# A queue of common PSUM banks, a fold cut in three, and a third bank for the last products

## The chip, the cores and the metric

The kernel runs on one core of one Trainium2 chip. The core has a matrix engine (PE, with a separate record PEld for its weight loads), a vector engine (DVE), a scalar engine (ACT), a general engine (POOL) and a queue engine (SP) that here issues nearly all transfers. PE writes its results into a memory of its own, PSUM, of which the kernel uses eight banks; DVE and ACT read them from there. The metric is the device time of one execution in microseconds.

## The reference, cut to what matters

The program computes a top-k attention and then a Fourier mixing block with a two-layer network. Everything is in 32-bit floats.

```python
scores = (1 / sqrt(64)) * q @ k^T                 # 8 batches, 8 heads, 576 x 576
kth = 32nd largest score of each row
attn = softmax(where(scores >= kth, scores, -1e9))
x = (attn @ v), heads side by side                # (8, 576, 512)

mixed = real(fft over 512 channels(fft over 576 tokens(x)))
u = x + mixed
un = (u - mean(u)) / sqrt(var(u) + 1e-6)
out = u + relu(un @ w_ch1) @ w_ch2                # 512 -> 2048 -> 512
```

## The kernel before, in words

**Steps and tiles.** The attention of the 32 pairs of heads is cut into 288 tiles, nine a pair and 36 a batch. The main loop at the end of the kernel takes one tile a step, in steps of about 6 us once it has settled. For tile i, DVE finds the 32 largest scores of each row with MAX8 and MATCH_REPLACE8 (`top_ops`, L384 and L386). POOL then forms two bounds from the first and last of them (`bounds`, L393, tile `nt`), ACT makes a mask (L400), POOL subtracts it from the scores (L401, tile `wk`), ACT takes the exponent (L407), PE transposes the result (L428, tile `tpP`), and matmuls with v follow (L465). These are spread over three consecutive steps: `bounds` of tile i in step i, mask and exponent in step i+1, transposes in step i+2.

**The second block rides along.** The Fourier mixing and the network of batch b are done while the attention of batch b+1 or b+2 runs. `at(step, where, fn)` books a piece of work for a place in a step. The list `queue` holds units of the network, and `some()` puts as many of them between the attention's matmuls as PE has room for by a cost in microseconds; only their order on PE is set by this, the semaphores do the rest. The units are, for each of two chunks of a batch (320 and 256 rows): 16 `hidden` units (L827, tile `hp`), then either plain products `back` (L854, tile `cp`; L893 for the 64 rows that are left over) or the seven products of a Strassen-Winograd scheme, `fast` (L1024, tiles `cv` and `cw`). Chunk 0 of batches 1 to 7 and chunk 1 of batch 7 are done by `fast`; batch 7 is the last.

**The common banks.** Three PSUM banks (pool `ps_m`) are shared by `hp`, `cp`, `cv`, `cw` and, in all but the last batch, by the transforms over tokens (`yp`, L629), over channels (`mp`, L677), the transposes before the network (`tpu`, L742) and some transposes of x (`tpx`, L505). The function `bank()` gives out the next one in turn, 0, 1, 2, 0, and so on. A tile that lives over many units is taken with `hold=True`; it is skipped in the turn until its `free` is called. A bank given out again while its former tile is still being read makes the new writer wait. In `back`, part 7 ends a `cp` tile: for row tile 2 ACT scales it into SBUF (L881), `free()` is called, and the next unit asks for the bank of row tile 3.

**The seven products.** In `fast`, two banks `v` and `w` are held. Each has a low and a high half of 256 columns. The products come as p2, p1, p5, p4, p6, p3, p7, each in two parts of four matmuls. p1, p6 and p7 add up in the low half of `w`; p4 is written into the high half of `w`. `to_x` adds a finished half to x: in the last batch directly from PSUM by DVE (L982), otherwise over ACT (L994) and POOL. `mix` (L969) makes sums of the hidden values on POOL, `bring` (L770) fetches parts of the second weight matrix over SP: p5 part n brings T2, which p6 part n uses.

**The fold.** Ahead of the transform over tokens, x is folded. `fold_tails(b, eng)` folds the 64 left-over rows of a batch: two adds of halves into `zt` (L566), then a memset, three copies and four adds into `ftail` (L550 to L562 and L575). For batches 1 to 6 it is booked as one call at place "pool0", which lies on POOL between the subtraction of tile i-1 (L401) and `bounds` of tile i (L393). `T0` is the step of the fold: the last step of the batch plus 3 for batch 1, plus 4 for batches 2 to 6. `fold_tails` stands at T0-1 for batch 1 and at T0 for batches 2 to 6; the large folds (`fold_ops`) follow from T0+1, and `yp` from T0+4 or T0+5.

Of the kernel before, what the change touches and what calls it, by code (L numbers as in the profile page):

```python
# [9 lines left out]
F32 = mybir.dt.float32  # L10
# [8 lines left out]
P = 128  # L19
# [45 lines left out]
def kernel(  # L65
# [9 lines left out]
    nc = tc.nc  # L75
    B, H, S, D = q.shape
    DM = H * D
# [5 lines left out]
    TAIL = 2 * TH  # L83
# [23 lines left out]
    batp = ctx.enter_context(tc.tile_pool(name="batp", bufs=1))  # L107
# [7 lines left out]
    ps_m = ctx.enter_context(tc.tile_pool(name="ps_m", bufs=3, space=bass.MemoryType.PSUM))  # L115


    held, turn = set(), [0]

    def bank(shape, name, hold=False):  # L120
        while turn[0] in held:
            turn[0] = (turn[0] + 1) % 3
        n = turn[0]
        turn[0] = (n + 1) % 3
        t = ps_m.tile(shape, F32, name=name, tag=f"m{n}", bufs=1)
        if not hold:
            return t
        held.add(n)
        return t, lambda: held.discard(n)

    ident = const.tile([P, P], F32, name="ident", tag="ident")
    fs = const.tile([P, 2, 2, 3, KQ], F32, name="fs", tag="fs")
# [11 lines left out]
    ftail = const.tile([P, DM + 1], F32, name="ftail", tag="ftail")  # L144
# [76 lines left out]
    x_of, o_of, xT_of, rd_of = ({} for _ in range(4))  # L221
# [322 lines left out]
    Q1, Q2, Q3 = DM // 4, DM // 2, 3 * DM // 4  # L544
    folded, y_of, yt_of, us_of, rs_of, unT_of = ({} for _ in range(6))

    def fold_channels(eng, z, f, n):

        def tt(out, up, down, op):
            eng.tensor_tensor(out=f[..., out], in0=z[..., up], in1=z[..., down], op=op)  # L550

        if n == 0:
            eng.memset(f[..., Q1:Q1 + 1], 0.0)
            eng.tensor_copy(out=f[..., 0:DM:Q2], in_=z[..., 0:DM:Q2])
            up, down = slice(1, Q1), slice(Q2 - 1, Q1, -1)
            tt(up, up, down, ALU.add)
            tt(slice(Q1 + 1, Q2), up, down, ALU.subtract)
        else:
            up, down = slice(Q2 + 1, Q3), slice(DM - 1, Q3, -1)
            tt(up, up, down, ALU.subtract)  # L560
            tt(slice(Q3, DM - 1), up, down, ALU.add)
            eng.tensor_copy(out=f[..., DM - 1:DM], in_=z[..., Q3:Q3 + 1])  # L562

    def fold_halves(eng, s_, z):
        for cols, op in ((slice(0, Q2), ALU.add), (slice(Q2, DM), ALU.subtract)):
            eng.tensor_tensor(out=z[..., cols], in0=s_[..., 0:Q2], in1=s_[..., Q2:DM], op=op)  # L566

    def fold_tails(b, eng):

        z = batp.tile([P, DM], F32, name=f"zt_{b}", tag="fold_s")[0:TAIL]  # L570
        f = ftail[0:TAIL]
        fold_halves(eng, x_of[b][0:TAIL, 4, :], z)
        for n in range(2):
            fold_channels(eng, z, f[:, 0:DM], n)
        eng.tensor_copy(out=f[:, DM:DM + 1], in_=z[:, Q1:Q1 + 1])  # L575

    def fold_ops(b, par, eng, space="own"):

# [234 lines left out]
    def mlp_units(b):  # L813
        x = x_of[b]
        last = b == B - 1
# [113 lines left out]
        def fast(ch):  # L929

            ta, tb = CHUNKS[ch][0], CHUNKS[ch][1]
# [12 lines left out]
            rs, banks = rs_of[b], {}  # L944
            lo, hi = slice(0, DH), slice(DH, DM)
# [8 lines left out]
            def room(n):  # L954
                return ct_tile().rearrange("p t c -> p (t c)")[:, DH * n:DH * (n + 1)]

            def later(key, us, fn, soon=False):

                n = sum(s[3] for s in sums) if soon else len(sums)
                sums.insert(n, ((b, ch, *key), us, fn, soon))  # L960
                if last:
                    need((b, ch, *key))
# [12 lines left out]
            def to_x(t, cols, src, n, then=lambda: None):  # L975


                xt = x[:, t, cols].rearrange("p (e c) -> p e c", c=DH)
                e = xt.shape[1]
                if n is None or last:  # L980
                    def add():
                        nc.vector.scalar_tensor_tensor(  # L982
                            out=xt,
                            in0=src.rearrange("p (e c) -> p e c", e=1).to_broadcast([P, e, DH]),
                            scalar=rs[:, t:t + 1], in1=xt, op0=ALU.mult, op1=ALU.add,
                        )
                        then()
                    if last:
                        add()
                    else:  # L990
                        late_next.append(add)
                    return
                r = room(n)
                nc.scalar.mul(out=r, in_=src, mul=rs[:, t:t + 1])  # L994
                xt = x[:, t, cols]
                later(("x", n), 0.75, lambda: nc.gpsimd.tensor_tensor(
                    out=xt, in0=xt, in1=r, op=ALU.add
                ))
# [20 lines left out]
            def product(name, cols, a, rhs_of, part, start):  # L1019


                dst = half_bank(name, cols)
                for kc in range(NK // 2 * part, NK // 2 * (part + 1)):
                    nc.tensor.matmul(  # L1024
                        dst, lhsT=h()[a][:, kc, :], rhs=rhs_of(kc), start=start and kc == 0,
                        stop=kc == NK - 1, skip_group_check=True,
                    )
                return dst
# [29 lines left out]
                    to_x(tb, hi, c, 2)  # L1058

            def p4(part):  # L1060
                c = product("w", hi, "22", in_second, part, False)
                bring(T3, second, part)
                if part:
                    to_x(tb, lo, c, 3)
                    mix("22", "22", "11")

            def p6(part):
# [92 lines left out]
    def at(step, where, fn, cost=0.0):  # L1160
        plan.setdefault((step, where), []).append(fn)
        costs[step] = costs.get(step, 0.0) + cost
# [68 lines left out]
    for o, place in ((B12, w2_12), (B21, w2_21)):  # L1231
        at(PER_BATCH + 14, "load2", lambda o=o, place=place: nc.sync.dma_start(
            out=scr[:, o], in_=place
# [3 lines left out]
    for b in range(B):  # L1237
        end = PER_BATCH * (b + 1) - 1
        last = b == B - 1
        first, soon = b == 0, b == 1  # L1240
        T0 = end + (2 if first else 3 if soon else 4)
        if first:

            at(T0 - 1, "pool", lambda b=b: fold_tails(b, nc.gpsimd))

            def folds(b=b):
                for par, space in ((0, "own"), (1, "hT")):
                    for op in fold_ops(b, par, nc.vector, space):
                        op()
            at(T0, "dve", folds)  # L1250
            ft, fc = (T0 + 1, T0 + 1), T0 + 1
        elif soon:

            at(T0 - 1, "pool0", lambda b=b: fold_tails(b, nc.gpsimd))
            for par in range(2):
                def folds(par=par, b=b, T0=T0):
                    for n, op in enumerate(fold_ops(b, par, nc.gpsimd)):
                        at(T0 + 1 + 3 * par + min(n, 2), "pool0", op)
                at(T0, "begin", folds)
            ft, fc = (T0 + 4, T0 + 7), T0 + 8  # L1260
        elif not last:
            at(T0, "pool0", lambda b=b: fold_tails(b, nc.gpsimd))
            for par in range(2):
                def folds(par=par, b=b, T0=T0):
                    for n, op in enumerate(fold_ops(b, par, nc.gpsimd)):
                        at(T0 + (6 if par else 1) + n, "pool0", op)
                at(T0, "begin", folds)
            ft, fc = (T0 + 5, T0 + 11), T0 + 12
        else:
            at(T0 - 1, "pool0", lambda b=b: fold_tails(b, nc.gpsimd))  # L1270

            def folds(b=b):
                for op in fold_ops(b, 0, nc.vector) + fold_ops(b, 1, nc.vector, "PT"):
                    op()
            at(T0, "dve", folds)

            at(T0 + 1, "pe1", lambda: one_unit() + one_unit() if len(queue) > 1 else 0.0)
            ft, fc = (T0 + 1, T0 + 3), T0 + 4
        for par in range(2):
            at(ft[par], "pe1", lambda b=b, par=par: dft_tokens(b, par), 4.3)  # L1280
        for n, t in enumerate((0, 1, 4, 2, 3)):
            quick = first or last
            s = fc + (0 if first else n // 3 if last else n // 2)
            at(s, "pe2", lambda b=b, t=t, q=quick: dft_channels(b, t, q), 1.75)
            if not quick:
                at(s, "pool2", lambda b=b, t=t: add_mixed(b, t))
                at(s + 1, "dve", lambda b=b, t=t: stats(b, t))
            at(s + (1 if quick else 2), "pe", lambda b=b, t=t: channels_first(b, t), 0.6)
            if first and t == 4:
                at(s + 1, "pe", lambda: (queue.extend(waiting), waiting.clear()) and 0.0)  # L1290
        at(s + 1, "begin" if quick else "dve", lambda b=b: rsqrt(b))
        arrivals.append(s + (1 if quick else 2))
        at(arrivals[-1], "units", lambda b=b: (queue if b else waiting).extend(mlp_units(b)))
# [43 lines left out]
    while i < N + 4 or plan or queue or sums:  # L1337
# [54 lines left out]
        cost, got = carry, 0.0  # L1392
# [38 lines left out]
        first, second = top_ops(i, (2, 3)), top_ops(i + 1, (0, 1))  # L1431
# [58 lines left out]
```

## Time and profile before

| what | value |
|---|---|
| median of 3 runs | 1923.65 us (1923.27 to 1925.76) |
| span of the profiled execution | 1923.6 us |
| PE busy | 1806.9 us, 94% of the span |
| DVE busy | 1585.2 us, 82% |
| ACT busy | 1210.0 us, 63% |
| POOL busy | 872.6 us, 45% |
| mean granted clock of PE | 0.973 |

All times within the run are microseconds from the start of the span. A line of the instruction listing gives the start, the time from the first to the last of a run of equal instructions, the engine, the line of the code, the operation, the tiles as out<-in with their shapes, and the number of instructions; in brackets stands the idle time of the engine before it and what ended it. A line of the list of waits gives who waited, for whom, the total, the number of times and the longest.

### The profile page before, as it was taken

How to read it: one execution, taken by the hardware profiler on the slowest of the kernel's cores; microseconds unless marked ns; L12 is line 12 of the kernel's file. 1: busy time of each engine (PE TensorE's matmuls, PEld its weight loads, DVE VectorE, ACT ScalarE, POOL GpSimd, SP SyncE). 2: the span in 40 equal slices, each digit the busy share in tenths (PEclk: the TensorE clock that was granted, in tenths of full speed). 3: DMA queues.
4: the chain of work that ended last, by engine and by line, in shares of the span. 5: the costliest groups of instructions: out<-in, count | busy, mean ns of one | idle time of the engine just before them, and what ended most of it. 6: DMA issues, size and time to landing. Idle time of an engine off the chain costs nothing.

```text
span 1923.6 us, 28279 instructions
## 1 busy us (share of the span) xinstructions
PE 1806.9 (94%) x9008; PEld 1195.3 (62%) x9008; DVE 1585.2 (82%) x3277; ACT 1210.0 (63%) x3078; POOL 872.6 (45%) x1158
## 2 busy tenths in 40 slices
PE   6567799999999999999999999999999999999999
PEld 3334465474666756667567656667567656767677
DVE  8999989999999998989899888888899988872110
ACT  6878657676766767656676667666676667652100
POOL 4768643545635364345535454345534454241012
PEclk8877899999999999999999999999999999999999
DMA  5333001220104111140013101140013102030132
GB/s 162 105 95 107 19 13 47 86 70 24 47 8 128 33 25 47 41 109 26 24 47 101 51 17 52 41 113 22 23 47 101 49 19 58 23 102 6 50 102 76
DMA packets 184339, 111.34 MB, mean 58 GB/s; under 512 B 125952, under 2 KB 174208, under 8 KB 184192
## 3 DMA queue, kind: packets, MB, share of 16 engines
q1 hardware_dynamic: 183408, 109.33, 20.0%
q8 instruction: 72, 1.18, 0.3%
q14 instruction: 75, 0.61, 0.1%
q10 hardware_dynamic: 784, 0.21, 0.0%
HBM read 93.76 MB, written 15.73 MB: 57 GB/s over the span
## 4 chain that ended last, share of the span: by engine, by line
PE 79%; POOL 6%; DVE 5%; ACT 4%; issue 3%; DMA 1%; SPq 0%; POOLq 0%; DVEq 0%; ACTq 0%
PE hp L827 25%; PE cp L854 11%; PE o L465 7%; PE sp L363 6%; PE tpP L428 5%; PE cw L1024 5%; PE cv L1024 4%; PE yp L629 3%; PE mp L677 3%; PE cp L893 3%; DVE m L384 3%; POOL wk L401 2%; DVE wk L386 2%; PE sp_t L333 2%; POOL w L215 1%
## 5 line engine op out<-in xcount | busy, mean ns | idle before, releaser
L401 POOL TENSOR_TENSOR wk<-S,wk 128x576 f32<-128x576 f32 x288 | 408.4, 1418 | 806.0 <-ACT wk L400 775.2
L384 DVE MAX8 m<-wk 128x8 f32<-128x576 f32 x864 | 623.3, 749 | 5.2
L827 PE MATMUL hp<-unT,w 128*128 128x256 f32 (+1 forms) x2048 | 538.3, 410 | 2.6 <-ACT unT L745 2.6
L827 PEld LDWEIGHTS hp<-unT,w 128*128 128x128 f32 x2048 | 373.6, 191 | 124.3 <-issue 24.2
L386 DVE MATCH_REPLACE8 wk<-m,wk 128x576 f32<-128x576 f32 x576 | 427.6, 742 | 0.0
L407 ACT ACTIVATE wk<-wk,nt 128x576 f32<-128x576 f32 x288 | 224.7, 780 | 66.4 <-POOL wk L401 65.5
L428 PE MATMUL tpP<-ident,wk 128*128 128x128 f32 x1152 | 184.6, 285 | 72.7 <-ACT wk L407 47.3
L854 PE MATMUL cp<-w,hT 128*128 128x512 f32 x512 | 242.6, 601 | 4.0 <-ACT hT L881 4.0
L431 ACT COPY PT<-tpP 128x512 f32<-128x512 f32 (+1 forms) x320 | 171.4, 546 | 118.8 <-PE tpP L428 116.4
L400 ACT ACTIVATE wk<-S,nt 128x576 f32<-128x576 f32 x288 | 226.9, 788 | 24.3 <-POOL nt L393 23.3
L428 PEld LDWEIGHTS tpP<-ident,wk 128*128 128x128 f32 x1152 | 141.6, 145 | 147.1 <-ACT wk L407 68.3
L831 ACT ACTIVATE hT<-hp 128x320 f32<-128x320 f32 (+1 forms) x256 | 104.9, 410 | 193.9 <-PE hp L827 191.8
L384 DVE MAX8 m<-S 128x8 f32<-128x576 f32 x288 | 214.0, 743 | 9.5 <-ACT S L337 9.4
L386 DVE MATCH_REPLACE8 wk<-m,S 128x576 f32<-128x576 f32 x288 | 213.7, 742 | 0.0
L465 PE MATMUL o<-PT,v 128*64 128x256 f32 (+3 forms) x1440 | 194.3, 412 | 1.5 <-ACT PT L431 1.4
L366 ACT COPY S<-sp 128x512 f32<-128x512 f32 (+1 forms) x264 | 141.9, 588 | 56.9 <-PE sp L363 56.5
L363 PE MATMUL sp<-kT,qT 64*128 64x512 f32 (+1 forms) x528 | 162.6, 675 | 4.3 <-ACT means L1210 3.3
L465 PEld LDWEIGHTS o<-PT,v 128*64 128x64 f32 x1440 | 111.1, 152 | 72.7 <-issue 15.8
L854 PEld LDWEIGHTS cp<-w,hT 128*128 128x128 f32 x512 | 89.0, 191 | 92.4 <-issue 85.7
L969 POOL TENSOR_TENSOR hT<-hT 128x512 f32<-128x512 f32 x64 | 81.5, 1276 | 101.1 <-ACT hT L831 89.4
L1024 PE MATMUL cw<-w,hT 128*128 128x256 f32 x448 | 106.5, 383 | 2.7 <-issue 1.4
L1024 PEld LDWEIGHTS cw<-w,hT 128*128 128x128 f32 x448 | 81.4, 190 | 20.3 <-issue 5.2
(140 smaller groups left out, 2150.2 us busy)
## 6 DMA issues: line engine op xcount, KB each, us to landing
w<-w_parts SPq DMA_DIRECT2D x82, 512.0 KB, 4.4
space<-in_moe_w_ch_dram SPq DMA_DIRECT2D x32, 512.0 KB, 3.5
nat<-in_q_dram SPq DMA_DIRECT2D x128, 64.0 KB, 2.2
v<-in_v_dram SPq DMA_DIRECT2D x128, 64.0 KB, 2.3
out_dram<-x SPq DMA_DIRECT2D x32, 256.0 KB, 2.1
nat<-in_k_dram SPq DMA_DIRECT2D x124, 64.0 KB, 2.2
w_parts<-w_t SPq DMA_DIRECT2D x8, 512.0 KB, 2.9
w_s<-w_parts SPq DMA_DIRECT2D x8, 512.0 KB, 4.9
```

Source lines behind the costliest of these rows:

```text
L363: nc.tensor.matmul(sp[r], lhsT=qT[hd, q_cols], rhs=kT[hd, :], start=True, stop=True)
L384: ops.append(lambda src=src, m8=m8: nc.vector.max(out=m8, in_=src))
L386: ops.append(lambda src=src, m8=m8: nc.vector.match_replace(w, m8, src, NEG))
L400: nc.scalar.activation(out=w, in_=Ssb[i], func=AF.Relu, scale=-FAR, bias=Nt[i][:, 1:2])
L401: nc.gpsimd.tensor_tensor(out=w, in0=Ssb.pop(i), in1=w, op=ALU.subtract)
L407: nc.scalar.activation(out=w, in_=w, func=AF.Exp, bias=Nt.pop(i)[:, 0:1], accum_out=den_t[pair % 3][:, c:c + 1],)
L428: nc.tensor.transpose(tp[:, c, :], p_sb[:, k0 + P * c:k0 + P * (c + 1)], ident)
L431: nc.scalar.copy(out=pt[:, NF * he:NF * (he + 1), col:col + w], in_=tp[:, :, o:o + w])
L465: nc.tensor.matmul(o[D * e:D * (e + 1), c0:c1], lhsT=vv[:, c, e, :], rhs=pt[:, 2 * NF if c == NF else NF * e + c, c0:c1], start=(c == 0), ...
L827: nc.tensor.matmul(hp[:, 0:w], lhsT=w1[:, dt, P * it:P * (it + 1)], rhs=unT[:, dt, 0:w], start=(dt == 0), stop=(dt == NDT - 1),)
L854: nc.tensor.matmul(cp, lhsT=hT[:, it, P * n:P * (n + 1)], rhs=w2[:, it, :], start=(it == 0), stop=(it == NIT - 1),)
L1024: nc.tensor.matmul(dst, lhsT=h()[a][:, kc, :], rhs=rhs_of(kc), start=start and kc == 0, stop=kc == NK - 1, skip_group_check=True,)
```

## The change

`bank()` keeps the free banks in a list: it takes the first, and a bank goes to the end of the list when it is given back, which for a tile taken without `hold` is at once. `fold_tails` returns three functions: the halves; the first half of the channels; the second half and the last copy. For batches 1 to 6 they are booked at T0-2, T0-1 and T0, one a step. For batches 0 and 7 all three stay in the step where the whole was. In the last batch p4 is written into a third held bank `z`, with the start flag on its first matmul, and `z` is given back when DVE has been told to add it to x.

Of the last two hunks of the diff the first is that of batch 1 and the second that of batches 2 to 6.

```diff
-    held, turn = set(), [0]
+    banks_free = [0, 1, 2]
     def bank(shape, name, hold=False):
-        while turn[0] in held:
-            turn[0] = (turn[0] + 1) % 3
-        n = turn[0]
-        turn[0] = (n + 1) % 3
+        n = banks_free.pop(0)
         t = ps_m.tile(shape, F32, name=name, tag=f"m{n}", bufs=1)
         if not hold:
+            banks_free.append(n)
             return t
-        held.add(n)
-        return t, lambda: held.discard(n)
+        return t, lambda: banks_free.append(n)
...
     def fold_tails(b, eng):
-        z = batp.tile([P, DM], F32, name=f"zt_{b}", tag="fold_s")[0:TAIL]
-        f = ftail[0:TAIL]
-        fold_halves(eng, x_of[b][0:TAIL, 4, :], z)
-        for n in range(2):
-            fold_channels(eng, z, f[:, 0:DM], n)
-        eng.tensor_copy(out=f[:, DM:DM + 1], in_=z[:, Q1:Q1 + 1])
+        f, got = ftail[0:TAIL], []
+        def first():
+            got.append(batp.tile([P, DM], F32, name=f"zt_{b}", tag="fold_s")[0:TAIL])
+            fold_halves(eng, x_of[b][0:TAIL, 4, :], got[0])
+        def third():
+            fold_channels(eng, got[0], f[:, 0:DM], 1)
+            eng.tensor_copy(out=f[:, DM:DM + 1], in_=got[0][:, Q1:Q1 + 1])
+        return [first, lambda: fold_channels(eng, got[0], f[:, 0:DM], 0), third]
...
             def p4(part):
-                c = product("w", hi, "22", in_second, part, False)
+                c = product("z" if last else "w", hi, "22", in_second, part, last)
                 bring(T3, second, part)
                 if part:
-                    to_x(tb, lo, c, 3)
+                    to_x(tb, lo, c, 3, lambda: banks["z"][1]())
...
-            at(T0 - 1, "pool0", lambda b=b: fold_tails(b, nc.gpsimd))
+            for n, op in enumerate(fold_tails(b, nc.gpsimd)):
+                at(T0 - 2 + n, "pool0", op)
...
-            at(T0, "pool0", lambda b=b: fold_tails(b, nc.gpsimd))
+            for n, op in enumerate(fold_tails(b, nc.gpsimd)):
+                at(T0 - 2 + n, "pool0", op)
```

More of the change, by code (lines that the diff above doesn't have):

```diff
@@ L1242 @@
         if first:
-            at(T0 - 1, "pool", lambda b=b: fold_tails(b, nc.gpsimd))
+            for op in fold_tails(b, nc.gpsimd):
+                at(T0 - 1, "pool", op)
             def folds(b=b):
@@ L1269 @@
         else:
-            at(T0 - 1, "pool0", lambda b=b: fold_tails(b, nc.gpsimd))
+            for op in fold_tails(b, nc.gpsimd):
+                at(T0 - 1, "pool0", op)
             def folds(b=b):
```

## The prediction

> **What bounds the kernel now.** I read four views in this order: the page (who is busy), the table by stage, the list of PE's waits, and the listing of instructions around each wait. The page and the table first:
>
> ```profile
> PE 1806.9 (94%) x9008; PEld 1195.3 (62%) x9008; DVE 1585.2 (82%) x3277; ACT 1210.0 (63%) x3078; POOL 872.6 (45%) x1158
> PE 79%; POOL 6%; DVE 5%; ACT 4%; issue 3%; DMA 1%; SPq 0%; POOLq 0%; DVEq 0%; ACTq 0%
> 0.00:250.00 250.00, 167.63 (x808) 103.34 (x809) 232.24 (x482) 187.31 (x441) 156.77 (x168) 0.81 0.31 94
> 250.00:800.00 550.00, 528.74 (x2661) 337.05 (x2660) 513.48 (x1058) 379.61 (x1000) 261.31 (x367) 0.99 0.17 47
> 800.00:1800.00 1000.00, 991.90 (x5030) 661.81 (x5029) 830.00 (x1722) 628.78 (x1603) 434.36 (x607) 1.00 0.19 53
> 1800.00:1924.00 124.00, 118.64 (x514) 93.09 (x512) 9.49 (x17) 14.30 (x34) 20.14 (x16) 1.00 0.22 71
> ```
>
> The first line is busy time by engine, the second the shares of the chain that ended last, the rest stages with PE, PEld, DVE, ACT and POOL. From 250 us on PE is the bound: 96% busy, then 99%, then 96%. Before 250 us DVE is (232 of 250), but nothing moves there: no bank is held before the first `back`, so both rules give 0, 1, 2, and batch 0 keeps its fold. A change that leaves PE's work alone can therefore win only PE's idle time after 250 us: 21.3 + 8.1 + 5.4 = 34.8 us. The order of PE's instructions is the same in both kernels except that p4 of the last batch goes to `cz`. So the question is which waits end.
>
> ```profile
> PE tpP L428 <- ACT wk L407: 10.8, 12, 3.7
> PE cp L854 <- ACT hT L881: 4.0, 4, 1.6
> PE tpu L742 <- ACT us L694: 1.5, 4, 0.4
> PE cw L1024 <- issue: 1.4, 3, 0.6
> ```
>
> These are PE's waits from 250 us to the end (total, times, longest). The second is a wait for a common bank, the first holds one wait of 3.7 us behind the fold, the last the two waits in the last batch. I take each to its place.
>
> [...] p6 (low half of `w`) starts at 1849.41, just after DVE's read of p4's high half (1848.83 + 0.48 = 1849.31). [...] matmuls that follow each other overlap by 0.16 us in the records (p4's start every 0.43, each 0.59 long), so a recorded gap costs 0.16 more than it shows; and `nt` stands behind a fold below. [...] the `cp` gap repeats once a batch.
>
> **Part 1, the queue of banks.** In batch 3:
>
> ```profile
> 1141.70 1.88 PE L854 MATMUL cp<-w,hT 128*128 128x512 f32 x4
> 1144.37 1.98 PE L854 MATMUL cp<-w,hT 128*128 128x512 f32 x4 [0.78 <-ACT hT L881]
> 1143.62 0.69 ACT L881 ACTIVATE hT<-cp,gi 128x512 f32<-128x512 f32 x1 [0.72 <-PE cp L854]
> ```
>
> Row tile 2 has just ended, ACT scales it out of its bank, and row tile 3 was given that very bank. Followed through the whole program, the two rules differ thus: `cp` of row tile 3 gets in batches 1 to 5 the bank of row tile 2 before, and after the change one whose last reader (L655, of `yp`) ended 10 to 21 us earlier. The four recorded gaps are 1.63 us (702.29, batch 1; ACT is late there, L881 runs 701.55 to 702.24) and 0.78 in batches 3, 4 and 5. In batch 2 row tile 3 starts at 927.11, after ACT was done, so nothing is won. With the overlap: 1.79 + 3 x 0.94 = **4.6 us**; the lower end is the gaps alone, 4.0. To see new waits I set, for every common bank after 250 us, the new predecessor's last read in this trace against the tile's first write. The four `tpu` waits stay (0.37 each, same predecessor `mp`); the closest new pair is `mp` of batch 1 at 498.38, 0.77 us after its new predecessor's last read. No wait is added.
>
> **Part 2, the fold in three.** Only batch 1 has a wait to win:
>
> ```profile
> 453.74 1.27 POOL L883 TENSOR_TENSOR x<-x,hT 128x512 f32<-128x512 f32 x1 [1.55 <-ACT hT L881]
> 454.97 1.41 POOL L566 TENSOR_TENSOR zt<-x 64x256 f32<-64x256 f32 x2
> 456.70 1.69 POOL L550 TENSOR_TENSOR ftail<-zt 64x127 f32<-64x127 f32 x4
> 458.59 0.18 POOL L393 TENSOR_TENSOR nt<-m,cc 128x2 f32<-128x2 f32 x1
> 458.81 0.78 ACT L400 ACTIVATE wk<-S,nt 128x576 f32<-128x576 f32 x1 [2.24 <-POOL nt L393]
> 462.02 0.66 PE L428 MATMUL tpP<-ident,wk 128*128 128x128 f32 x4 [3.68 <-ACT wk L407]
> ```
>
> DVE had the maxima for this `nt` at about 453.1, but POOL did the fold first, 3.6 us. After, the halves (1.4 us) stand a step earlier and the second half of the channels plus copies a step later. Between L883 (end 455.0) and `nt` remain memset, copy and two adds: from the listing 456.32 to 456.70 plus 2 x 0.42, so 1.2 us, and `nt` starts at 456.2. ACT's earlier work (L366) ends at 456.56, so L400 starts there, 2.2 us earlier. From L400 to PE it stays 3.2 us, so PE starts at 459.8, and 1.5 of its 3.7 us remain: **2.2 us** won. The third piece, 1.2 us, sits a step later between a subtraction that is itself 2.2 us earlier and its `nt`; that `nt` starts at about 460.1 instead of 461.02. The first piece delays the `nt` of 445.17 by 1.4 us; ACT used it at 449.92 (4.6 us of slack). DVE must follow: it idles 2.3 us at 473.8 to 476.1 for PE to give back `wk`, which shrinks. Bounds: nothing, if another wait refills it, to 2.4, the whole time that leaves POOL's queue ahead of that `nt`.
>
> In batches 2 to 6 the same pieces cost POOL nothing new but stand in two more steps. Behind them waits `nt`, and for it L400. Slack from `nt` to L400 was 1.87 to 3.6 us at T0-2 (the halves take 1.4) and 1.87 at T0-1 (1.2), and a further 3.2 to 4.5 us from the exponent to PE. So cost nothing; nothing to win either, PE has no gap at T0+1 or T0+2 there. The halves wait for DVE's normalised tail rows, in batch 3 done at 852.7, 13 us before POOL comes to them (866.5).
>
> **Part 3, bank `z`.**
>
> ```profile
> 1848.83 0.48 DVE L982 SCALAR_TENSOR_TENSOR x<-cw,gi,x 128x256 f32<-128x256 f32 x1 [2.97 <-PE cw L1024]
> 1849.41 3.69 PE L1024 MATMUL cw<-w,hT 128*128 128x256 f32 x16 [0.63 <-issue]
> 1909.29 1.97 PE L1024 MATMUL cw<-w,hT 128*128 128x256 f32 x8 [0.62 <-issue]
> 1843.64 2.10 SPq L770 DMA_DIRECT2D w<-w_parts  x2
> ```
>
> With p4 in `z`, p6 waits only for DVE's read of p1, over at 1842.4. It could start at 1848.62, 0.79 us earlier. But its second part needs the second T2 transfer, issued at 1845.36 and landed 5.2 us later, 1850.60 (view of the tile `w`, landings 3.9 to 5.2). PE starts 0.04 after such a landing (1709.91 to 1709.95), so at 1850.64 instead of 1851.21: 0.57 won of 0.79. In chunk 1 the landing is 1910.43 (5.2 again): 1910.47 instead of 1911.09, 0.62. Together **1.2 us**, all on the path that ends; bounds 0.4 (a transfer 0.4 slower each time) and 1.6 (no wait for it). `z` itself is the bank of the last `hidden`, read by ACT over 6 us before; no cost. DVE and SP have the same instructions in the same order.
>
> **Sum.** 4.6 + 2.2 + 1.2 = 8.0 us off the span of 1923.6. That execution's span is at the median of the timed runs (1923.65), so 1923.65 - 8.0 = **1915.7 us**.
>
> **Rivals.**
> - *DVE takes back what is won before 800 us.* For: DVE is 93% busy from 250 to 800. Against: it idles 2.3 us at 476 and 5.0 at 728.9 waiting for PE. Then parts 1 (1.79) and 2 (2.2) are lost, 4.0 remain: 1919.7.
> - *More comes with it.* The waits at 746 to 760 us (0.53 + 0.35 + 1.16 + 1.05 = 3.1) follow from the same step's order and may close: 1912.6.
> - *Parts do not do what they say*: the fold's wait refills, and the late T2 eats `z`: 4.6 + 0 + 0.4 with half of part 1 lost too gives about 1921.
> - *Slower.* In batches 2 to 6 the first piece blocks POOL's queue at T0-2, with `nt` behind it. PE notices only after 1.9 + 4.5 = 6.3 us (batch 2) or about 8.0 (3.6 + 4.5, later ones). To end 0.2% above before, five batches must lose 8.0 + 3.9 us, 2.4 each, so a block of some 10 us: 1927.5. The tail rows' 13 us of lead speak against it.
>
> **How the numbers follow.** 0.2% is 3.85 us, about what a measurement of this kernel can tell from no change. Chances: all three parts 0.66 (own range 1913.5 to 1918), DVE 0.15, more 0.08, parts that fail 0.07, slower 0.04. The border lies at 1919.8, so DVE's case counts half as faster: faster 0.66 + 0.08 + 0.08 = 0.82, same 0.14, slower 0.04. The range 1912.5 to 1920 leaves out the last two and half of "more".
>
> **What would show it.** No wait of `cp` for ACT L881; four `tpu` waits of 0.37 still there; the gap near 462 at about 1.5 us; in the last batch `cw` with no gap of 0.6 at p6's start and one of about 0.3 (or none) in its middle; busy times unchanged. I am wrong if PE's idle time after 250 us falls by less than 5 us, or if new waits for `nt` or for banks appear.

## The result and the profile after

The changed kernel took 1914.47 us in the median of 4 runs (1912.67 to 1916.72), beside 1924.7 us of the kernel before in 4 runs (1923.27 to 1926.89): a ratio of 0.9946, with a 95% interval from 0.9929 to 0.9964. A second set of five runs gave 0.9959 (0.9946 to 0.9971). The forecast was 1915.7 us, 8.0 us less than before.

The page of the changed kernel gives the span and the busy times, in the form of the first line shown of before:

```profile
span 1910.9 us, 28281 instructions
PE 1802.4 (94%) x9008; PEld 1195.1 (63%) x9008; DVE 1584.9 (83%) x3277; ACT 1208.4 (63%) x3078; POOL 870.5 (46%) x1158
```

The counts of instructions on these engines are those of before. PE's busy time fell by 4.5 us all the same, which no part of the change intends; that is the first hint that the 12.7 us between the two profiled spans (1923.6 and 1910.9) are not all the change's. The table by stage (PE, PEld, DVE, ACT, POOL, then the granted clock) shows idle PE after 250 us: 17.4 + 5.5 + 3.7 us, the last counted to the end of this span at 1910.9. That is 26.6 us, where 34.3 stood when before is counted to the end of its span too.

```profile
250.00:800.00 550.00, 532.60 (x2702) 340.92 (x2701) 520.57 (x1074) 383.80 (x1013) 264.87 (x371) 1.00 0.17 48
800.00:1800.00 1000.00, 994.46 (x5029) 664.21 (x5028) 823.11 (x1707) 625.03 (x1595) 429.40 (x603) 1.00 0.19 53
1800.00:1924.00 124.00, 107.23 (x473) 85.47 (x472) 8.74 (x16) 12.54 (x30) 20.11 (x16) 0.99 0.21 69
```

PE's waits from 250 us on (total, times, longest), the lines that answer to those shown of before and one more:

```profile
PE tpP L426 <- ACT wk L405: 8.6, 13, 2.3
...
PE tpu L746 <- ACT us L698: 1.5, 4, 0.4
PE cw L1028 <- POOL nt L391: 1.2, 3, 0.4
...
PE cw L1028 <- issue: 0.2, 1, 0.2
```

The four waits of `cp` for ACT are gone. The longest wait of `tpP` is 2.3 instead of 3.7. Its count is 13 instead of 12: a wait of 0.18 near 355 us is new in this execution, where the matmuls around it ran at full clock and not at half; e2 and e8 below have 12 again. The four `tpu` waits are as forecast. The two waits of 0.6 in the last batch are gone; the third of that line, 0.2 in batch 2, is left.

The three places in the listing of instructions. The bank, in batch 3:

```profile
1143.18 3.60 PE L858 MATMUL cp<-w,hT 128*128 128x512 f32 x8
```

Row tiles 2 and 3 are now one run of eight matmuls, where before a group of four took 1.88, a gap followed, and the next four took 1.98. The fold, in batch 1:

```profile
452.06 0.86 POOL L548 TENSOR_TENSOR ftail<-zt 64x127 f32<-64x127 f32 x2
452.89 0.18 POOL L391 TENSOR_TENSOR nt<-m,cc 128x2 f32<-128x2 f32 x1
452.32 1.07 ACT L364 COPY S<-sp 128x512 f32<-128x512 f32 x2 [0.57 <-PE sp L361]
453.28 0.79 ACT L398 ACTIVATE wk<-S,nt 128x576 f32<-128x576 f32 x1
456.50 0.66 PE L426 MATMUL tpP<-ident,wk 128*128 128x128 f32 x4 [1.34 <-ACT wk L405]
```

`nt` (L391) starts 0.8 us after the adds of the second piece begin, and L398 carries no bracket: ACT goes to it straight from its own copies (L364), not from a wait for `nt`. PE's gap is 1.34, where 3.68 stood. The last batch:

```profile
1834.14 3.62 PE L1028 MATMUL cz<-w_s,hT 128*128 128x256 f32 x16
1837.60 3.71 PE L1028 MATMUL cw<-w,hT 128*128 128x256 f32 x16
1837.80 0.48 DVE L986 SCALAR_TENSOR_TENSOR x<-cz,gi,x 128x256 f32<-128x256 f32 x1 [2.97 <-PE cz L1028]
```

p6 (`cw`) starts while p4 (`cz`) is still to be read by DVE.

**Where the 12.7 us came from.** PE runs the same 9008 matmuls in the same order, so each can be set against itself in the other trace, and the difference of the two starts moves in steps. Before 460 us it had already reached 3.18 us, in a part of the program where the change ends no wait of PE. Then came 2.34 at the fold's place (462.0 us of before), 1.90, 1.05, 1.04 and 1.05 at the `cp` tiles of row tile 3 in batches 1, 3, 4 and 5, and 0.86 at p6 in each chunk of the last batch, of which 0.10 was lost again in the middle of the first. These sum to **9.0 us**; about 0.5 more came in small steps, the largest of them, 0.24, at the landing of another transfer (1709.95 us of before).

Most of the first 3.18 us are matmuls at half speed: 1.70 near 260 us and 1.29 near 350. The table by stage around 260 us, before and then after:

```profile
258.00:262.00 4.00, 1.92 (x12) 1.30 (x11) 3.86 (x12) 2.77 (x8) 1.99 (x10) 1.00 0.00 0
262.00:266.00 4.00, 4.00 (x10) 2.60 (x9) 3.93 (x8) 0.44 (x1) 3.58 (x9) 0.57 0.00 0
```

```profile
258.00:262.00 4.00, 1.92 (x11) 1.34 (x10) 3.86 (x12) 2.61 (x8) 2.15 (x11) 1.00 0.00 0
262.00:266.00 4.00, 4.00 (x22) 3.00 (x21) 3.93 (x8) 1.11 (x3) 3.59 (x9) 1.00 0.00 0
```

From 262 to 266 us PE got through 10 matmuls in the one execution and 22 in the other, at a granted clock of 0.57 and 1.00. The same happened near 351 us. The experiments had to show whether that belongs to the change.

### The profile page after: what moved, and what is told of

It is laid out like the page before. It is cut to its first block, busy times and chain, and to the rows that moved or that the text cites. A ratio compares the mean times of both kernels' runs of the same rounds, so it can differ in the third digit from the quotient of the medians.

```text
span 1910.9 us, 28281 instructions
## 1 busy us (share of the span) xinstructions
PE 1802.4 (94%) x9008; PEld 1195.1 (63%) x9008; DVE 1584.9 (83%) x3277; ACT 1208.4 (63%) x3078; POOL 870.5 (46%) x1158
## 4 chain that ended last, share of the span: by engine, by line
PE 80%; POOL 8%; ACT 4%; issue 3%; DVE 2%; DMA 1%; SPq 0%; POOLq 0%; ACTq 0%; DVEq 0%
PE hp L831 25%; PE cp L858 10%; PE o L463 8%; PE sp L361 6%; PE tpP L426 5%; PE cw L1028 5%; PE cv L1028 4%; PE yp L633 3%; PE mp L681 3%; POOL wk L399 3%; PE cp L897 3%; POOL w L213 2%; POOL w L212 2%; PE sp_t L331 2%; DVE m L382 1%
## 5 line engine op out<-in xcount | busy, mean ns | idle before, releaser
L405 ACT ACTIVATE wk<-wk,nt 128x576 f32<-128x576 f32 x288 | 224.7, 780 | 68.1 <-POOL wk L399 64.1
L398 ACT ACTIVATE wk<-S,nt 128x576 f32<-128x576 f32 x288 | 226.9, 788 | 22.6 <-POOL nt L391 21.5
L364 ACT COPY S<-sp 128x512 f32<-128x512 f32 (+1 forms) x264 | 141.7, 588 | 54.2 <-PE sp L361 54.1
```

The source lines that it names most:

```text
L398: nc.scalar.activation(out=w, in_=Ssb[i], func=AF.Relu, scale=-FAR, bias=Nt[i][:, 1:2])
L405: nc.scalar.activation(out=w, in_=w, func=AF.Exp, bias=Nt.pop(i)[:, 0:1], accum_out=den_t[pair % 3][:, c:c + 1],)
```

## The experiments

My theory: three independent gains of about 5.0, 2.3 and 1.6 us in the records, the rest chance of the clock. The rivals: one part does all; the parts help each other; the fold's gain comes from the cut and not from the place; 12.7 us is what the change is worth. "Before" is run beside each set.

| run | kernel | us (median, lowest to highest) | ratio to before (95%) |
|---|---|---|---|
| e1 | queue alone | 1920.16 (1917.71 to 1923.56) | 0.9978 (0.9970 to 0.9986) |
| e2 | fold alone | 1920.14 (1918.76 to 1925.40) | 0.9985 (0.9977 to 0.9992) |
| e3 | bank z alone | 1923.61 (1921.63 to 1926.97) | 0.9994 (0.9986 to 1.0002) |
| e4 | changed, old bank for row tile 3 | 1919.66 (1917.17 to 1923.76) | 0.9979 (0.9971 to 0.9987) |
| e5 | changed, fold uncut and early | 1915.87 (1915.39 to 1918.65) | 0.9951 (0.9938 to 0.9964) |
| e6 | changed, fold three times | 1955.90 (1954.09 to 1958.16) | 1.0152 (1.0136 to 1.0168) |
| e7 | changed, z in all batches | 1913.16 (1911.87 to 1915.63) | 0.9934 (0.9921 to 0.9947) |
| e8 | changed, again | 1917.61 (1916.57 to 1919.81) | 0.9959 (0.9946 to 0.9971) |
| e9 | e7 with long filling | 1913.43 (1912.65 to 1914.50) | 0.9944 (0.9931 to 0.9956) |
| e10 | e7 again | 1912.43 (1910.92 to 1915.07) | 0.9936 (0.9923 to 0.9950) |
| e11 | e7 with short filling | 1912.85 (1911.61 to 1913.68) | 0.9933 (0.9919 to 0.9946) |
| e12 | e7 a third time | 1912.93 (1911.92 to 1916.24) | 0.9938 (0.9925 to 0.9950) |

e1 to e4 shared a chip, e5 to e8 another set of runs of before, and so did e9 with e10 and e11 with e12.

### One part at a time: e1, e2, e3

e1 is the kernel before with the first hunk of the diff alone (`bank()` with its list), e2 with `fold_tails` in three and its bookings alone, e3 with these two lines alone:

```diff
-                c = product("w", hi, "22", in_second, part, False)
+                c = product("z" if last else "w", hi, "22", in_second, part, last)
...
-                    to_x(tb, lo, c, 3)
+                    to_x(tb, lo, c, 3, lambda: banks["z"][1]())
```

> The kernel before with the queue of banks alone. Theory A (each removed wait is worth what PE's starts moved by at its place, and nothing else is won): 5.0 us, in four steps at the cp tiles of row tile 3, 1.8 in batch 1 and about 1.05 in batches 3, 4 and 5; the gap of 3.7 us near 462 us and the two of 0.6 in the last batch stay. Ratio about 0.9974. Theory B (most of the measured 10 us comes from the order of the banks in general): 8 us or more. Theory C (DVE takes back what is won early): the step of batch 1 is given back before 800 us and only 3.2 us remain.

> The kernel before with the fold in three pieces alone. Theory A: 2.4 us, in one step at the transpose of tile 73 near 460 us, where a gap of about 1.3 us remains; the four waits of cp for its bank and the two gaps of the last batch stay; no new wait in batches 2 to 6. Ratio about 0.9988. Theory C: the step near 460 is given back within the next 100 us, where DVE has little idle time, and nothing is left at the end. A gain that is spread over batches 2 to 6 would contradict both.

> The kernel before with the third bank for p4 of the last batch alone. Theory A: 1.6 us, 0.78 at p6 of each chunk of the last batch, nothing before it. Ratio about 0.9992. Theory D (my recorded forecast: the second T2 transfer limits it): 0.57 and 0.62, so 1.2 us, with a wait of about 0.25 us in the middle of p6. What decides is the landing of that transfer after its issue: 5.2 us gives D, 4.9 us or less gives A.

In e1 PE's starts gain 1.90, 1.05, 1.05 and 1.05 us at the four `cp` tiles, 5.05 us, and nothing at the fold or in the last batch. Its profiled span, 1921.5 us, is only 2.1 us below that of before, because this execution had two more stretches at half clock, near 463 and 487 us (a granted clock of 0.57 in the 4 us from 463 and from 487). Its list of waits keeps the long wait that the fold would end:

```profile
PE tpP L425 <- ACT wk L404: 10.7, 12, 3.7
```

In e2 the starts gain 2.34 us at the transposes of tile 73, where the gap of 3.68 us stood, and nothing at the banks; the list of waits is the mirror image of e1's:

```profile
PE tpP L429 <- ACT wk L408: 8.4, 12, 2.3
PE cp L861 <- ACT hT L888: 4.0, 4, 1.6
```

In e3 p6 of chunk 0 gains 0.86 us against before (0.79 at its start) and loses 0.37 in its middle, where its second part waits for the transfer of T2; p6 of chunk 1 gains 0.86 and loses nothing. The products of chunk 0 in e3 (start, first to last, number of matmuls):

```profile
1844.98 3.62 PE L1024 MATMUL cz<-w_s,hT 128*128 128x256 f32 x16
1848.43 3.99 PE L1024 MATMUL cw<-w,hT 128*128 128x256 f32 x16
```

Sixteen matmuls that run through take 3.62; p6's 3.99 are the 0.37 more. By the ratios the parts are worth 4.2, 2.9 and 1.2 us, 8.3 together, and the product of the three ratios, 0.9957, lies between the two measurements of the whole (0.9946 and 0.9959). The interval of e3 includes 1, so by its times alone part 3 is not shown; the steps of the trace show it. Within these intervals the parts add up, and none needs another.

### The old bank back: e4

The changed kernel, but row tile 2's bank goes to the head of the list when it is given back, so that row tile 3 gets it, as before:

```diff
-        return t, lambda: banks_free.append(n)
+        return t, lambda first=False: banks_free.insert(0, n) if first else banks_free.append(n)
...
-                        free()
+                        free(t == 2)
```

> The changed kernel, except that the bank of row tile 2 goes to the head of the list when it is given back, so that row tile 3 takes it again as in the kernel before; all else is a queue. Theory A: the four waits for ACT return, 1.6 and three of 0.78 us, and the kernel is 5.0 us slower than the changed one, so 4.0 us faster than before by the traces' steps. Theory B (the order of the other takes matters too): less than 3 us of loss against the changed kernel.

The one bank brings back the four waits, to the number, in the list of PE's waits:

```profile
PE cp L858 <- ACT hT L885: 4.0, 4, 1.6
```

In e4's steps the fold (2.34) and z (0.86 in each chunk, less 0.31 in the first) are there, those of `cp` are not, and the time is 0.9979 instead of 0.9946 and 0.9959. So the queue's worth is these four tiles and nothing else of its new order.

### The cut or the place: e5

The changed kernel with the fold uncut: whole at T0-2 in batch 1, whole at T0 in batches 2 to 6.

```diff
-            for n, op in enumerate(fold_tails(b, nc.gpsimd)):
-                at(T0 - 2 + n, "pool0", op)
+            for op in fold_tails(b, nc.gpsimd):
+                at(T0 - 2, "pool0", op)
```

(and with `T0` in the second place).

> The changed kernel, with the fold uncut: in batch 1 the whole of it stands one step earlier than before the change (step T0-2, where only the first piece stands in the changed kernel), in batches 2 to 6 the whole stands at T0 as before the change. Theory 'it is the place': the 2.3 us at tile 73 came because the fold left the queue ahead of that tile's bounds. At T0-2 the whole fold (3.6 us) delays the bounds of the tile before, which ACT uses 4.6 us after they were ready, so nothing more is lost: the gap before the transposes of tile 73 is about 1.3 us as in the changed kernel, and the time within 0.1% of the changed kernel (about 1915 us; before 1924.7). Rival 'it is the cut': the whole fold at T0-2 brings the long wait back one tile earlier, at about 455 us: the longest wait of the transposes for the exponent is again above 3 us and the time is about 2 us above that of the changed kernel (1917).

POOL, ACT and PE in e5:

```profile
446.36 0.18 POOL L577 COPY ftail<-zt 64x1 f32<-64x1 f32 x1
446.49 0.19 POOL L391 TENSOR_TENSOR nt<-m,cc 128x2 f32<-128x2 f32 x1
...
447.63 0.78 ACT L398 ACTIVATE wk<-S,nt 128x576 f32<-128x576 f32 x1
...
457.39 0.66 PE L426 MATMUL tpP<-ident,wk 128*128 128x128 f32 x4 [1.34 <-ACT wk L405]
```

The whole fold delays this `nt` to 446.68, still 0.95 us before ACT comes to it at 447.63 without waiting. The gap at tile 73 is 1.34, as in the changed kernel. Place alone brings it; in batch 1 the cut is not needed.

### How much room POOL had: e6

The changed kernel, but in batches 2 to 6:

```diff
-            for n, op in enumerate(fold_tails(b, nc.gpsimd)):
-                at(T0 - 2 + n, "pool0", op)
+            for _ in range(3):
+                for op in fold_tails(b, nc.gpsimd):
+                    at(T0 - 2, "pool0", op)
```

> The changed kernel, but in batches 2 to 6 the whole fold is done three times over (the same values) in the one step T0-2: some 11 us on POOL ahead of the bounds of one tile, where the changed kernel has 1.4. It prices the slack that the prediction gave the fold in these batches: 1.9 + 4.5 = 6.3 us in batch 2 and 3.6 + 4.5 = about 8 us in batches 3 to 6 between POOL and PE. Theory 'slack as counted': one new wait of PE for the exponent in each batch, about 4.5 us in batch 2 and 3 us in batches 3 to 6, together some 16 us, unless DVE's lead catches part of it: 1925 to 1932 us. Rival 'no slack': PE loses the whole extra 9.6 us in each of five batches, 48 us in all: about 1963 us. Rival 'far more slack': PE loses nothing, about 1915 us; then the first piece could never have hurt.

Between the theory and the rival of no slack, nearer to the rival: 1955.9 us, 38 more than the changed kernel in the same set (e8). The wait is not where I had put it. PE's list of waits, then the listing in batch 3 (POOL, ACT and PE):

```profile
PE tpx L503 <- ACT xT L477: 28.3, 5, 7.2
```

```profile
1105.70 0.18 POOL L391 TENSOR_TENSOR nt<-m,cc 128x2 f32<-128x2 f32 x1
1105.92 0.77 ACT L398 ACTIVATE wk<-S,nt 128x576 f32<-128x576 f32 x1 [7.41 <-POOL nt L391]
...
1108.20 0.78 ACT L405 ACTIVATE wk<-wk,nt 128x576 f32<-128x576 f32 x1 [0.76 <-POOL wk L399]
...
1108.98 0.35 ACT L477 COPY xT<-o 128x256 f32<-128x256 f32 x1
...
1109.38 0.69 PE L503 MATMUL tpx<-ident,xT 128*128 128x128 f32 x2 [5.21 <-ACT xT L477]
```

Here PE does not wait for the exponent's result but for `xT`, a copy of an earlier tile that stands behind that exponent (L405) in ACT's queue. The extra 9.7 us on POOL became gaps of 7.2, 5.5, 5.2, 5.2 and 5.2 us of PE in batches 2 to 6. So the room beyond the first piece was 2.5 us in batch 2 and 4.2 to 4.5 in the others, where my count had given 4.9 and 6.6 (6.3 and 8.0 less the 1.4 of that piece). In the changed kernel's trace it can be read off: `nt` is ready at 1074.83 and used at 1077.08 (2.25), ACT idles 0.49 ahead of `xT`, which ends at 1081.13, and PE takes it at 1082.69 (1.56): 4.3 us. Of the other 12 us between the spans of e6 and e8 (1956.4 and 1915.8) most is matmuls at half speed, which follow each of the five gaps: the eight `hp` matmuls after the gap shown took 3.51 us, where eight take 1.89.

### One more bank: e7, and the changed kernel again: e8

In the changed kernel p6 still waits for 0.39 us in batches 3, 4 and 5. e7 puts p4 into `z` in all batches:

```diff
-                c = product("z" if last else "w", hi, "22", in_second, part, last)
+                c = product("z", hi, "22", in_second, part, True)
```

and calls `then()` after ACT's scaling in the branch of the earlier batches. e8 is the changed kernel without an edit.

> The changed kernel, with p4 in the third held bank z in batches 1 to 6 too (given back once ACT has scaled it). In the changed kernel p6 of batches 3 to 5 still starts with a gap of 0.39 us in the records, and batches 1, 2 and 6 with less. Two things end within 0.1 us of each other ahead of it: ACT's read of p4 from the other half of the same bank (end 1038.16 in batch 3) and POOL's sum for p6 (end 1038.10). Theory 'the bank': the gaps close, with the overlap of the records about 3 x 0.55 + 0.4 = 2 us won, about 1912.5 us, and no new wait for a bank. Rival 'the sum': POOL's sum holds p6 at the same moment, the gaps stay within 0.1 us of 0.39, and the time is within 0.5 us of the changed kernel.

> The changed kernel again, on the same chip and beside the same runs of the kernel before, for the comparison with the three others and for a second execution of its profile. Theory: 8.9 us of its gain are the three parts (five waits at banks and one behind the fold), and the rest of the 12.7 us between the first two profiled spans were matmuls that ran at a lower clock in the one execution; then the ratio of many runs is near 1 - 8.9 / 1924 = 0.9954, the gaps of this second profile are those of the first, and its slow stretches of matmuls lie elsewhere or are fewer or more. Rival: 12.7 us were won by the change; then the ratio is near 0.9934, and the steps of PE's starts against the kernel before sum to 12.7 again.

p6 in batch 3, of the changed kernel and of e7, and in e7 POOL's sum and ACT's read of p4:

```profile
1038.26 1.97 PE L1028 MATMUL cw<-w,hT 128*128 128x256 f32 x8 [0.39 <-POOL nt L391]
```

```profile
1036.00 1.89 PE L1029 MATMUL cz<-w,hT 128*128 128x256 f32 x8
1037.08 1.27 POOL L973 TENSOR_TENSOR hT<-hT 128x512 f32<-128x512 f32 x1
1037.93 0.47 ACT L998 ACTIVATE ct<-cz,gi 128x256 f32<-128x256 f32 x1
1037.95 1.89 PE L1029 MATMUL cw<-w,hT 128*128 128x256 f32 x8
```

In e7 p6 starts at 1037.95, while both are still going on (to 1038.35 and 1038.40), so its first part needed neither POOL's sum nor ACT's read, only the bank. The name in the changed kernel's bracket, POOL's `nt`, was the wrong one. PE's starts gain 0.41, 0.62, 0.62, 0.62 and 0.30 us against the changed kernel in batches 2 to 6, 2.6 us. The profiles of e7 and e8 lie further apart, 5.8 us; of these 2.8 were there before 455 us, where e8 had its two stretches at half clock and e7 none, and 0.4 are of the last batch. So the 4.5 us between their medians are not to be read as the worth of this bank. With 0.9934, and 0.9936 and 0.9938 in e10 and e12, this is the best version here, about 12 us under the kernel before.

In e8's profile PE's starts gain 2.34, then 1.90, 1.05, 1.04 and 1.04, and 0.86 at each p6, but p6 loses 0.68 and 0.57 again in its middle, for T2. Its sum is 7.8 us against the same profiled execution of before, 0.9959 as a ratio, which is what the five runs gave. This time the two stretches at half clock, near 260 and 350 us, are in both traces. So the 3.18 us are not the change's.

### When the clock fell: e9 to e12

The stretches at half clock are all alike. Read in slices of 0.1 us, from 250 to 520 us and over twelve traces (without the two with filling), they begin between 261 and 264 or near 350, 463, 484 or 487 us and last 3.4 to 3.5 us at a granted clock of 0.50, and each follows a gap of PE of 1.9 to 3.7 us. In the 3.4 us just ahead of one, as long a time as a stretch lasts, PE was busy for 0.31 to 0.44 of the time. Some executions, that of the changed kernel among them, have none.

In the profile of before the two stretches run from 262.1 to 265.5 us and from 350.8 to 354.2, with PE busy for 0.39 and 0.44 of the 3.4 us ahead. Within the first, matmuls of `hp` start every 0.53 us, and every 0.27 outside it; its 16 `hp` matmuls took 6.27 us instead of the 4.57 of the changed kernel, 1.7 us more.

The gap near 260 us does not decide it alone. PE waits there for 2.1 us in all twelve traces (258.74 to 260.82 in before, 258.59 to 260.66 after). In seven of them half clock follows, with PE busy for 0.39 of the 3.4 us ahead; in five, after among them, the clock stays at 1.00. What makes the difference is not shown here.

e9 is e7 with matmuls that nobody reads, ahead of three places where PE waits about 2 us in every trace:

```diff
+    def fill(name):
+        t = ps_m.tile([P, DM], F32, name=f"fill_{name}", tag=f"m{banks_free[0]}", bufs=1)
+        for _ in range(3):
+            nc.tensor.matmul(t, lhsT=ident, rhs=w1[:, 0, 0:DM], start=True, stop=True)
...
+            if (b, ch, it) == (0, 0, 0):
+                fill("hp")
...
+        if i in (52, 77):
+            fill(f"tpP_{i}")
```

e11 does it with less: one matmul of 256 columns at the first place, three at the others. e10 and e12 are e7 without an edit.

> The kernel with p4 in z in all batches, and beside it three matmuls of 512 columns whose result nobody reads, into the free bank that is next in turn, ahead of three places where PE always waits about 2 us before 500 us: the first hidden unit of batch 0 (near 260 us), the transposes of tile 52 (near 350) and those of tile 77 (near 480). They take about 1.5 us of each gap, so PE is never idle for more than about 1 us there. In some executions so far the granted clock fell to 0.5 for some 3.4 us just after these places (260 to 266, 350 to 356 and 484 to 488 us), in others not. Theory 'the gap slows the clock': with the gaps filled the clock stays at 1.00 in all three places, the executions lie closer together (within some 2 us of one another instead of 4 to 5), and the median is 1 to 3 us below that of the same kernel without filling. Rival 'chance that has nothing to do with the gaps': slow stretches appear as often as before, the spread is the same and the time is equal within 0.5 us, or up to 1 us longer where the filling is in the way.

> The kernel with p4 in z in all batches again, on the same chip as the filled one. Theory: 2.4 us below the changed kernel in the middle batches, so about 0.9940 of the kernel before (1 - (8.9 + 2.4) / 1924); its executions spread over 4 to 5 us, the slower ones with half clock after the places near 260 and 350 us. Rival: the 0.9934 of its first five runs was luck with the clock, and it repeats the changed kernel's 0.9946 to 0.9959.

> The filled kernel with less filling: one matmul of 256 columns ahead of the first hidden unit of batch 0 (near 260 us) and three of 256 columns ahead of the transposes of tiles 52 and 77 (near 350 and 480 us), where the first had three of 512 columns, which ran 2.7 us each time and were longer than the gaps; from its records they put PE back by some 3 us. A matmul of 512 columns took two passes of 0.43 us, so one of 256 takes 0.43 us in all and three take 1.3 us, within gaps of 1.9 to 2.3 us. Theory 'the gap slows the clock': the clock stays at 1.00 at all three places again, now with nothing put back, so the time is about that of the best executions of the unfilled kernel: 1911 us (0.9930 of the kernel before), spread 2 us. Rival 'nothing to gain': the time is 1912.5 to 1913.5 with a spread of 4 us, and half clock still follows one of the places.

> The unfilled kernel (p4 in z in all batches) on the same chip, beside the one with less filling. Theory: 0.9935 of the kernel before once more, with a spread of some 4 us, and half clock after the place near 260 or 350 us in the slower executions. Rival: equal to the one with less filling within 0.5 us, in median and in spread.

In e9 the clock stayed at 1.00 from 225 us to beyond 480, but my filling was twice too long (2.7 to 2.8 us each time, six records that start 0.43 apart) and put PE back by about 3 us; the time is equal to e10's within 1 us. In e11 the fillings at tiles 52 and 77 fit, and no half clock followed there. At 260 us it did, for the filling itself had to wait for a bank:

```profile
259.71 0.70 PE L132 MATMUL fill_hp<-w,ident 128*128 128x256 f32 x2 [1.32 <-ACT unT L756]
260.56 6.23 PE L840 MATMUL hp<-unT,w 128*128 128x320 f32 x16
```

PE was busy for 0.57 of the 3.4 us ahead of that stretch, and the 16 `hp` matmuls took 6.23 us. The times show no gain of the filling: 1912.85 against 1912.93 us on the same chip. The five runs with it spread over 1.9 (e9) and 2.1 us (e11), those without over 3.8, 4.2 and 4.3 (e7, e10, e12); that speaks for the theory, but five runs each are few. What keeps the clock at 1.00 is not shown: half clock followed PE busy for 0.31 to 0.44 of the 3.4 us ahead in the twelve traces, but also for 0.57 in e11.

## Why the prediction was right

**Part 1, the queue.** Right in place and in kind: four waits gone, none added, batch 2 untouched, the four `tpu` waits unchanged. 5.0 us instead of 4.6, in every trace that has the queue without e4's edit. Each of the four terms was 0.1 too small: 1.90 instead of 1.79, and 1.04 to 1.05 instead of 0.94 (a gap of 0.78 and 0.16 of lost overlap: `cp`'s matmuls start every 0.43 and are 0.59 long in the records; p4's, to which the prediction gave those two figures, start every 0.22 and are 0.38 long, the same 0.16). A group of four that starts after a gap takes 1.98 against 1.88, which the lines of before that I had copied already showed.

**Part 2, the fold.** 2.2 us forecast, 2.33 to 2.34 in the nine profiles where it stands early and PE's matmuls are those of before, all at tile 73; the gap is 1.34 and not 1.5. That ACT's own earlier work would end last and not `nt` was right, and e5 shows the consequence: moving it was enough. In batches 2 to 6 the two further steps cost nothing, as said.

**Part 3, bank `z`.** 1.2 us forecast, with 0.4 to 1.6 as bounds. p6 always gains 0.86 (0.79 at its start); what is left of it is set by the second T2 transfer, as the step said. In the nine traces that have `z` and the matmuls of before, 0.0 to 1.6 us were left, 0.9 in the mean: 1.62 in the first profile, 1.35 in e3, 1.41 in e4, 0.47 in e8, 0.23 in e5, nothing in e6. So the mechanism was right, and 1.2 lies within the scatter that the landing of T2 makes; the lower bound, 0.4, was too high. In the first profile the transfer landed 4.9 and 4.6 us after its issue instead of 5.2, and 0.1 was lost; in e5 it came 5.8 us after its issue in chunk 0, and 0.97 was lost there.

**The rivals.** DVE took nothing back: after 462 and 702 us the lead of PE's starts stays to the end. Nothing more came with it: there is no step near 750 us. The parts did not fail. The slower case didn't come either, but its price was wrong: it counted 4.5 us from the exponent to PE behind the slack of `nt`, and the trace of the changed kernel shows about 2 (0.49 + 1.56), because another copy behind that exponent on ACT is needed earlier. By an estimate from e6 (the 1.4 us of the first piece and a room beyond it of 4.2 to 4.5 us, in batch 2 of 2.5), PE begins to wait at a block of some 6 us on POOL, not 8, and in batch 2 of some 4, not 6.3.

**What the sum left out.** The clock. A single pair of profiled spans gave 12.7 us, 3.0 of them from two stretches at half clock that only the one execution had; 8.0 was nearer to what both sets of runs say (10.2 and 8.8 us in the medians, 7.8 to 9.0 in the records) than that one difference. That it lies so near 7.8 is luck in part: part 1 was 0.4 too low, and part 3 was 0.4 too low in the first profile but 0.7 too high in e8. The prediction also set a span beside times: the execution with the span of 1923.6 us took 1925.34 us, so that its span equals the median time, 1923.65, is chance. Taking 8.0 off that median was sound all the same.

## What to carry to other kernels

A wait was priced here by what stood behind the waiting instruction on its engine, not by its own consumer: in batch 3 of e6 PE lost 5.2 us to `xT`, a copy that ACT made after the late exponent. Follow each later instruction on that engine to who needs it first. When two traces hold the same instructions in the same order, set each start against its twin; the steps of the difference give each part of a change its own number and leave chance aside. Look at who still reads a bank when it is handed out again: one whose last reader was still at work cost row tile 3 1.0 to 1.9 us each time, and one whose last reader had ended 10 to 21 us earlier cost it nothing.

## What was not expected of the hardware

- Gaps of PE of about 2 us were followed in some executions (seven of twelve near 260 us) by 3.4 to 3.5 us at a granted clock of 0.50, worth 1.7 and 1.3 us at the first two places. Two such stretches, 3.0 us, are a third of what the change itself won.
- Restarting after a wait cost 0.1 us beyond the lost overlap of 0.16 us, for four matmuls of 512 columns (1.98 against 1.88, and the steps of 1.04 to 1.05 where gap and overlap make 0.94).
- The second transfer of T2 landed 4.3 to 5.8 us after its issue in the same two places of the program, which moved the end of this kernel by up to 1.6 us (1.62 against nothing left of part 3).
